# Three Strassen sums and a border's small work moved in a fused retention and two-layer kernel, and the second product's matmuls put behind every second Strassen product

## The chip, the cores and the metric

One Trainium2 chip, one of its cores. The metric is device time in microseconds (us) from launch to end; lower is better. Engines in this text: TensorE (PE, matmuls; PEld its weight loads), VectorE (DVE), ScalarE (ACT), GpSimd (POOL) and SyncE (SP, which issues most DMAs). Matrix results land in PSUM, which has eight banks here called 0 to 7.

## The reference, cut to what matters

```python
B, H, S, D = 4, 8, 576, 64              # 4*576 = 2304 tokens, width 512
scores = q @ k.T / sqrt(D)              # per head
ret = scores * decay(head, i - j)       # retention: a causal decay mask
x = merge_heads(ret @ v)                # (2304, 512)

h = x @ w_in                            # (2304, 2048), first layer
x = relu(h) ** 2 @ w_out                # (2304, 512)

h = x @ w_in2                           # second layer
g = h * clip(h + 3, 0, 6) / 6
out = g @ w_out2                        # (2304, 512)
```

The four weight matrices come in 64-bit floating point; the kernel decodes them on the chip.

## The kernel before

**Precision and passes.** Each operand is split into a high and a low part, so that each product is three passes: high by high, high by low, low by high (`PASSES`). A "low" is always a VectorE or GpSimd subtraction behind a ScalarE copy that makes the "high".

**Stages.** First the retention (until about 60 us), whose result lies in `xall`, feature by token. Then the first layer on the first 768 tokens, directly: 16 steps `c` (`NCH = 16`), each a slice of 128 of the 2048 hidden features. After these come five blocks of 768 tokens (`BLOCKS`; layer 0 for tokens 768 and 1536, then layer 1 for all three), each of which goes through eight pairs of slices (`NPAIR = 8`), 40 pairs `k` in all. In these blocks the first product is made by a Strassen scheme with seven products.

**The first 768 tokens.** In step `c` TensorE runs `emit_h(c)` (24 matmuls into banks 6 and 7, L431) and then the second product of two steps earlier, `firsts(c - 2)` (24 matmuls, L478, in four steps of three 128x512 and three 128x256 ones). ScalarE empties banks 6 and 7 by `relu` (L447), squares (L450) and copies the high part (L451); `emit_h(c + 1)` may not write a bank before its `relu` is done. VectorE makes the low parts (L454) and does the long part of decoding the weights: clamp (L175, L178), `second` (L184), `third` (L190; the name of its tile tells what it is: `w...` for w_in, `wd` for w_out). A decoded slice of w_in is split for `emit_h(c + 2)` by ScalarE (L196) and GpSimd (L197), one of w_out likewise by `split_out`. At odd `c`, `sum_lefts` (L508 to L511) makes the left operands of the Strassen products on VectorE and sends them to DRAM.

**The border to the first Strassen block.** Right operands: four differences T1 to T4 of pieces of `xall` (`sums`, two VectorE operations of 128x384 each, L585), seven high parts on ScalarE (`highs`, L602, two operations each) and seven low parts on VectorE (`lows`, L607). The first pair's left operands for `e` = 2 and 3 are split by `parts_of_left` (L196 on ScalarE, L197 on VectorE).

**A pair.** `pair` runs the seven products in the order P1, P6, P2, P7, P5, P4, P3 (L690, six 128x384 matmuls each), alternately on banks `ta` and `tb` (7 and 6, swapped from pair to pair). P2 adds onto P1's bank after ScalarE has copied P1 out (L725); P7 takes P6's bank after VectorE has made `u2` from it (L714); P4 adds onto P7's bank and P3 onto P5's, each after the L714 on it. The four results become the hidden activations `g` of the pair: in layer 0 by ScalarE (L701, L702, L708) and the low part by VectorE (L710); in layer 1 with L706 and L707 ahead of them. The low part of a result is emitted behind the next product's L714 (`late`, `flush`).

**What stands between the products.** `between(i)` is called after the seven products, `i` = 0 to 6. It emits the matmuls of the second product of the pair before (`pending`, 8 steps in layer 0, L478 with tiles `yps` and `ytail`; 12 steps of three 128x512 matmuls in layer 1, L650), then the side work `side[i]`: loads, the next block's operands, and one "slot" of decoding the second layer's weights (`ready_slots`). The pending steps are those of `e` = 1 first; they need that half's `g`, whose last part comes from P4 of the pair before.

All engines run their instructions strictly in the order in which they are emitted; the lines below are emitted by hand in that order. Nothing is scheduled at run time.

## Time and profile before

| | |
|---|---|
| median of 3 runs | 845.2 us (844.39 to 845.39) |
| profiled execution | 845.26 us, of which the span from first to last instruction is 843.5 us |
| busy: PE / DVE / ACT / POOL | 825.0 / 586.1 / 466.6 / 144.5 us |
| granted TensorE clock | 0.999 of full speed, which is the level of 2.4 GHz |
| DMA | 245 GB/s on average |

A row of the timeline gives the start of a group of equal instructions, how long they were busy, and, in brackets, how long the engine had been idle before and what released it. Matmuls overlap, so the time that TensorE spends on a group is read as the start of the next group less its own start, not as its busy time.

### The profile page before, as it was taken

What the parts mean: (1) busy time and instruction counts of PE and PEld (TensorE: products, weight loads), DVE (VectorE), ACT (ScalarE), POOL (GpSimd) and SP (SyncE); (2) the same over time, 40 slices, a digit from 0 to 9 for tenths busy, and PEclk for the clock granted to TensorE, in tenths of its full rate; (3) what the DMA queues carried; (4) which work ended last, traced back from release to release, by engine and by line L of the source; (5) the groups of instructions that cost most, each with busy time, mean ns of one, the idle gap of its engine ahead of it and who ended that gap; (6) DMA issues with size and microseconds to landing.
All of it is one profiled execution on the core that took longest, in us unless ns stands there. A gap on an engine that the chain in (4) does not pass through costs nothing.

```text
span 843.5 us, 14173 instructions
## 1 busy us (share of the span) xinstructions
PE 825.0 (98%) x5220; PEld 741.9 (88%) x5220; DVE 586.1 (69%) x1018; ACT 466.6 (55%) x913; POOL 144.5 (17%) x122
## 2 busy tenths in 40 slices
PE   8989999997999999999999999999999999999998
PEld 7878888886999899999999888898898888889886
DVE  5779999999787876887875895546644546534434
ACT  1248777768865876867775653335433345433332
POOL 2353333331332320132230130000000000000000
PEclk9999999999999999999999999999999999999999
DMA  9996788876787894689786688553854552854522
GB/s 364 343 300 221 239 289 282 294 249 242 258 326 275 304 330 177 232 280 362 276 293 266 225 287 312 202 185 137 316 221 163 188 199 87 329 209 161 201 99 75
DMA packets 77963, 206.58 MB, mean 245 GB/s; under 512 B 8005, under 2 KB 24773, under 8 KB 77895
## 3 DMA queue, kind: packets, MB, share of 16 engines
q1 hardware_dynamic: 77314, 204.90, 68.9%
q8 instruction: 41, 0.67, 0.3%
q10 hardware_dynamic: 580, 0.79, 0.3%
q14 instruction: 28, 0.22, 0.1%
HBM read 159.00 MB, written 46.66 MB: 244 GB/s over the span
## 4 chain that ended last, share of the span: by engine, by line
PE 80%; DVE 7%; DMA 6%; ACT 4%; issue 1%; SPq 1%; POOL 0%; DVEq 0%; ACTq 0%; POOLq 0%
PE hps L690 33%; PE yps L650 22%; PE yps L478 13%; PE ytail L478 7%; PE hps L431 5%; DMA kvt<-in_kv_dram 3%; DMA qkt<-in_qk_dram 3%; DVE a L184 1%; DVE g L454 1%; DMA stage<-in_w_out_dram 1%; DVE w L190 1%; DVE a L178 1%; ACT u L706 0%; ACT r L172 0%; DVE u L714 0%
## 5 line engine op out<-in xcount | busy, mean ns | idle before, releaser
L650 PE MATMUL yps<-wo,g 128*128 128x512 f32 x864 | 226.8, 394 | 1.5 <-DVE g L710 1.3
L690 PE MATMUL hps<-xlast,win 128*128 128x384 f32 x960 | 194.9, 338 | 1.7 <-DVE u L714 1.6
L650 PEld LDWEIGHTS yps<-wo,g 128*128 128x128 f32 x864 | 159.4, 188 | 26.0 <-DVE g L710 2.0
L690 PEld LDWEIGHTS hps<-xlast,win 128*128 128x128 f32 x960 | 167.7, 188 | 10.5 <-DVE u L714 2.1
L714 DVE TENSOR_TENSOR u<-hps,u 128x384 f32<-128x384 f32 x120 | 66.8, 557 | 157.1 <-PE hps L690 150.5
L478 PE MATMUL yps<-g,wo 128*128 128x512 f32 x576 | 166.1, 396 | 0.4 <-POOL wo L197 0.4
L690 PE MATMUL hps<-xop,win 128*128 128x384 f32 x720 | 146.4, 338 | 3.7 <-ACT r L447 3.4
L690 PEld LDWEIGHTS hps<-xop,win 128*128 128x128 f32 x720 | 125.7, 188 | 10.7 <-ACT r L447 3.6
L708 ACT ACTIVATE g<-c 128x384 fp32r<-128x384 f32 x120 | 63.1, 525 | 88.1 <-DVE c L707 86.6
L478 PEld LDWEIGHTS yps<-g,wo 128*128 128x128 f32 x576 | 101.8, 188 | 10.2 <-POOL wo L197 0.8
L478 PEld LDWEIGHTS ytail<-g,wo 128*128 128x128 f32 x576 | 94.0, 188 | 17.3
L478 PE MATMUL ytail<-g,wo 128*128 128x256 f32 x576 | 98.5, 279 | 0.0
L710 DVE TENSOR_TENSOR g<-c,g 128x384 fp32r<-128x384 f32 x120 | 67.9, 566 | 11.3 <-ACT g L708 11.1
L431 PE MATMUL hps<-xring,win 128*128 128x512 f32 (+1 forms) x384 | 69.7, 338 | 0.3 <-ACT r L447 0.2
L733 ACT ACTIVATE c<-hps 128x384 f32<-128x384 f32 x40 | 19.7, 492 | 90.9 <-PE hps L690 90.9
L431 PEld LDWEIGHTS hps<-xring,win 128*128 128x128 f32 x384 | 60.1, 190 | 8.7 <-ACT r L447 0.7
L706 ACT ACTIVATE u<-c,three 128x384 f32<-128x384 f32 x72 | 44.4, 617 | 31.7 <-DVE c L714 30.5
L714 DVE TENSOR_TENSOR c<-hps,u 128x384 f32<-128x384 f32 x80 | 44.3, 554 | 21.8 <-PE hps L690 21.7
L184 DVE SCALAR_TENSOR_TENSOR a<-stage,a 128x512 int32<-128x512 int32 x64 | 51.2, 800 | 0.9
L707 DVE SCALAR_TENSOR_TENSOR c<-u,c 128x384 f32<-128x384 f32 x72 | 41.3, 574 | 13.5 <-ACT u L706 13.4
L171 ACT ACTIVATE a<-stage 128x512 f32<-128x512 f32 x64 | 42.4, 663 | 6.4 <-DMA stage<-in_w_in_dram 6.4
L172 ACT ACTIVATE r<-stage 128x512 int32<-128x512 uint32 x64 | 42.2, 660 | 0.0
(97 smaller groups left out, 905.5 us busy)
## 6 DMA issues: line engine op xcount, KB each, us to landing
win<-kept SPq DMA_DIRECT2D x88, 512.0 KB
wo<-kept SPq DMA_DIRECT2D x80, 512.0 KB
kept<-ready SPq DMA_DIRECT2D x40, 512.0 KB
win<-kept SPq DMA_DIRECT2D x72, 256.0 KB
stage<-in_w_out_dram SPq DMA_DIRECT2D x32, 512.0 KB
kept<-wo SPq DMA_DIRECT2D x16, 512.0 KB
stage<-in_w_in_dram SPq DMA_DIRECT2D x16, 512.0 KB
qkt<-in_qk_dram SPq DMA_DIRECT2D x13, 512.0 KB
```

Source lines behind the costliest of these rows:

```text
L171: nc.scalar.activation(out=a, in_=high.bitcast(F32), func=ACTF.Abs)
L172: nc.scalar.activation(out=r, in_=low.bitcast(U32), func=ACTF.Copy, scale=2.0 ** -29)
L184: nc.vector.scalar_tensor_tensor(out=a.bitcast(I32), in0=high, scalar=-0x40000000, in1=a.bitcast(I32), op0=ALU.bitwise_and, op1=ALU.bitwis ...
L431: nc.tensor.matmul(out=h, lhsT=w[:, kk // 2, wp, kk % 2 * 128:][:, :128], rhs=xs[kk][xp][:, o:o + n], start=m == 0, stop=m == 3 * KD - 1,)
L478: nc.tensor.matmul(out=p, lhsT=w[:, wp, m * 128:m * 128 + 128], rhs=gt[:, gpart, o:o + n], start=first and e == 0 and not (k and m % 2), s ...
L650: nc.tensor.matmul(out=p, lhsT=gt[:, gpart, m * 128:m * 128 + 128], rhs=w[:, wp], start=first and e == 0, stop=last and e == 2,)
L690: nc.tensor.matmul(out=to, lhsT=wl[k][:, half if k != 1 else 0, wp, o], rhs=x[:, xp, f], start=first and m == 0, stop=last and m == 5, ski ...
L706: nc.scalar.activation(out=v, in_=c, func=ACTF.Relu, bias=three)
L707: nc.vector.scalar_tensor_tensor(out=c, in0=v, scalar=6.0, in1=c, op0=ALU.min, op1=ALU.mult)
L708: nc.scalar.activation(out=hi, in_=c, func=ACTF.Copy)
L710: lambda: nc.vector.tensor_tensor(out=lo, in0=c, in1=hi.bitcast(F32), op=ALU.subtract)
L714: nc.vector.tensor_tensor(out=out_, in0=to, in1=x, op=ALU.add)
```

## The change

Four things are edited.

1. In the 16 steps: T1, T2 and T3 are emitted at the ends of steps 4, 6 and 8 in place of 11, 12 and 13.
2. Steps 13 to 15 and the border: `highs[0]` stands ahead of `split_in(15)` in place of the end of step 13; in step 14 the second w_out decode in hand is finished ahead of `emit_g(14)`; of the two left operands one is split at steps 14 and 15 and the other behind `highs[4]` and `lows[4]`; the last `sum_lefts` goes from step 15 to the end of the border.
3. In the first pair, T4 is emitted at `between(1)` in place of `between(0)`, `highs[5]` and `lows[5]` one place later, and slots begin at `between(3)`, so that the decoding of the second layer's weights, with its loads, stands three places later from there on.
4. In all 40 pairs the second product's steps stand only at those `between(i)` for which 7k + i is odd: behind every second product, counted over all pairs. A pair with even k has three groups of them (after P6, P7 and P4), one with odd k four (after P1, P2, P5 and P3).

```diff
--- before.py
+++ after.py
@@ -931,7 +931,6 @@
         def firsts(c):
             return ywork(wouts[c], g[c], c == 0, c == NCH - 1)
 
-        left_lows = []
 
         def sum_lefts(p):
             whole = left_sums(*(first_in[p][:, e] for e in range(2)), nc.vector)[1]
@@ -952,11 +951,15 @@
                 next_load()
             for d in dec:
                 d.pop(0)()
+            if c == NCH - 2:
+                for d in dec:
+                    for f in d:
+                        f()
+                    next_load()
+                dec = []
             if c == NCH - 1:
                 lows[1]()
-                for f in left_lows:
-                    f()
-                sum_lefts(p)
+                left[0][1]()
             if c > 1:
                 emit_g(c, h)
             for d in dec:
@@ -977,6 +980,8 @@
                 due.append(decode(*halves.pop(0)[1:]))
             for d in due[:1]:
                 d.pop(0)()
+            if c == NCH - 3:
+                highs[0]()
             if c and c + 2 < NCH:
                 split_in(c + 2)
             if c % 2 and c < NCH - 1:
@@ -989,18 +994,14 @@
                 keep(("o", 0, c - LAG), wouts[c - LAG].rearrange("p e n -> p (e n)"))
             if c == NCH - 5:
                 load_left(0)
-            if NCH - 5 <= c < NCH - 2:
-                for f in sums[2 * (c - NCH + 5):][:2]:
+            if c in (4, 6, 8):
+                for f in sums[c - 4:][:2]:
                     f()
-            if c == NCH - 3:
-                highs[0]()
             if c == NCH - 2:
                 highs[1]()
                 lows[0]()
-                for e in (2, 3):
-                    high, low = parts_of_left(0, e)
-                    high()
-                    left_lows.append(low)
+                left = [parts_of_left(0, e) for e in (2, 3)]
+                left[0][0]()
         assert not halves and not due
         pending = firsts(NCH - 2) + firsts(NCH - 1)
         highs[2]()
@@ -1008,7 +1009,10 @@
         lows[2]()
         highs[4]()
         lows[3]()
+        left[1][0]()
         lows[4]()
+        left[1][1]()
+        sum_lefts(NPAIR - 1)
         store_late()
         for c in (NCH - 2, NCH - 1):
             keep(("o", 0, c), wouts[c].rearrange("p e n -> p (e n)"))
@@ -1044,8 +1048,8 @@
                 if j:
                     side[0].append(lows[4])
                 else:
-                    side[0] += sums[6:]
-                for i, at in ((5, 1), (6, 3)):
+                    side[1] += sums[6:]
+                for i, at in ((5, 1 if j else 2), (6, 3)):
                     side[at].append(highs[i])
                     side[at + 1].append(lows[i])
             for i, e in ((4, 1), (6, 0)):
@@ -1057,7 +1061,7 @@
                     for n in range(2):
                         side[i + n].append(lambda e=e, n=n: parts_of_left(k + 1, e)[n]())
             if p < NPAIR - 1:
-                for i in range(4 if j and not p else 0, 7):
+                for i in range(0 if p else 4 if j else 3, 7):
                     if slots:
                         side[i] += [store_late] + slots.pop(0)
             elif late_stores:
@@ -1065,7 +1069,11 @@
             count = len(pending)
 
             def between(i):
-                want = count - count * (i + 1) // 7
+                groups = [n for n in range(7) if (7 * k + n) % 2]
+                if i not in groups:
+                    want = count
+                else:
+                    want = count - count * (groups.index(i) + 1) // len(groups)
                 while len(pending) > want:
                     pending.pop(0)()
                 for f in side[i]:
```

On VectorE, in step 4 of the first 768 tokens (a piece of the difference; `t` is T1's tile):

```order
 L184 SCALAR_TENSOR_TENSOR a<-stage,a 128x512
 L190 ISA w_1327<-a,r 128x1024
+L585 TENSOR_TENSOR t<-xall 128x384 x2
 L175 TENSOR_SCALAR a<-a 128x512
 L178 TENSOR_SCALAR a<-a 128x512
```

T1's two subtractions now stand ahead of the decoding of step 5; T2 and T3 are put in likewise at steps 6 and 8.

On VectorE, the last rows ahead of the first pair's L714 for P6 (`u<-hps,u`), before:

```order
L197 TENSOR_TENSOR win<-win 128x512 x2
L508 TENSOR_TENSOR sums<-w_2119 128x256
L509 TENSOR_TENSOR sums<-sums,w_2119 128x256
L510 TENSOR_TENSOR sums<-w_2119 128x256
L511 TENSOR_TENSOR sums<-w_2119,sums 128x256
L454 TENSOR_TENSOR g<-r,g 128x512
L454 TENSOR_TENSOR g<-r,g 128x256
L607 TENSOR_TENSOR xop<-xall,xop 128x384 x2
L607 TENSOR_TENSOR xlast<-xall,xlast 128x384 x2
L607 TENSOR_TENSOR xlast<-t,xlast 128x384 x2
L585 TENSOR_TENSOR xall<-xall,t 128x384 x2
L714 TENSOR_TENSOR u<-hps,u 128x384
```

and now:

```order
L454 TENSOR_TENSOR g<-r,g 128x512
L454 TENSOR_TENSOR g<-r,g 128x256
L607 TENSOR_TENSOR xop<-xall,xop 128x384 x2
L607 TENSOR_TENSOR xlast<-xall,xlast 128x384 x2
L607 TENSOR_TENSOR xlast<-t,xlast 128x384 x2
L197 TENSOR_TENSOR win<-win 128x512
L508 TENSOR_TENSOR sums<-w_2127 128x256
L509 TENSOR_TENSOR sums<-sums,w_2127 128x256
L510 TENSOR_TENSOR sums<-w_2127 128x256
L511 TENSOR_TENSOR sums<-w_2127,sums 128x256
L714 TENSOR_TENSOR u<-hps,u 128x384
L585 TENSOR_TENSOR xall<-xall,t 128x384 x2
```

One left operand's low part (`win`) and `sum_lefts` went behind the low parts of P2, P7 and P5 (`xop`, `xlast`), and T4 (`xall<-xall,t`) went from ahead of the L714 to behind it.

On TensorE, the pair k = 8, the first of the second block of layer 0 (its P1, P6 and P2 read `xop`, the others `xlast`), before:

```order
L690 MATMUL hps<-xop,win 128x384 x6
L478 MATMUL yps<-g,wo 128x512 x3
L478 MATMUL ytail<-g,wo 128x256 x3
L690 MATMUL hps<-xop,win 128x384 x6
L478 MATMUL yps<-g,wo 128x512 x3
L478 MATMUL ytail<-g,wo 128x256 x3
L690 MATMUL hps<-xop,win 128x384 x6
L478 MATMUL yps<-g,wo 128x512 x3
L478 MATMUL ytail<-g,wo 128x256 x3
L690 MATMUL hps<-xlast,win 128x384 x6
L478 MATMUL yps<-g,wo 128x512 x3
L478 MATMUL ytail<-g,wo 128x256 x3
```

and now:

```order
L690 MATMUL hps<-xop,win 128x384 x12
L478 MATMUL yps<-g,wo 128x512 x3
L478 MATMUL ytail<-g,wo 128x256 x3
L478 MATMUL yps<-g,wo 128x512 x3
L478 MATMUL ytail<-g,wo 128x256 x3
L690 MATMUL hps<-xop,win 128x384 x6
L690 MATMUL hps<-xlast,win 128x384 x6
L478 MATMUL yps<-g,wo 128x512 x3
L478 MATMUL ytail<-g,wo 128x256 x3
L478 MATMUL yps<-g,wo 128x512 x3
L478 MATMUL ytail<-g,wo 128x256 x3
L478 MATMUL yps<-g,wo 128x512 x3
```

A product that stood alone between two steps of the second product now runs right behind another (x12 is two products, one pair of rows `xop` x6 and `xlast` x6 too), and the second product's steps stand two or three together.

## Rows read from the trace of the kernel before

**Rows 1.** Busy time in two stretches (start:end, length, then busy us of each engine).

```profile
core 0: us, PE busy (x) PEld busy (x) DVE busy (x) ACT busy (x) POOL busy (x), PEclk, DMA share, GB/s
85.00:182.00 97.00, 96.79 (x557) 84.92 (x555) 93.54 (x141) 72.56 (x139) 35.57 (x23) 1.00 0.82 275
182.00:203.30 21.30, 15.84 (x85) 13.38 (x85) 20.30 (x37) 14.93 (x32) 4.46 (x3) 1.00 0.53 196
```

**Rows 2.** PE's timeline: `emit_h(15)`, P1 and P7 of the first pair.

```profile
181.98 4.45 PE L431 MATMUL hps<-xring,win 128*128 128x512 f32 x24 [0.21 <-ACT r L447]
...
194.70 1.31 PE L690 MATMUL hps<-xop,win 128*128 128x384 f32 x6 [3.43 <-ACT r L447]
...
203.27 1.32 PE L690 MATMUL hps<-xlast,win 128*128 128x384 f32 x6 [1.56 <-DVE u L714]
```

**Rows 3.** PE's timeline, end of pair 11 and begin of pair 12, layer 0.

```profile
385.43 1.23 PE L690 MATMUL hps<-xlast,win 128*128 128x384 f32 x6
386.49 0.87 PE L478 MATMUL yps<-g,wo 128*128 128x512 f32 x3
...
387.55 0.85 PE L478 MATMUL yps<-g,wo 128*128 128x512 f32 x3
...
388.59 1.21 PE L690 MATMUL hps<-xop,win 128*128 128x384 f32 x6
389.63 0.63 PE L478 MATMUL yps<-g,wo 128*128 128x512 f32 x2
```

**Rows 4.** PE's timeline, pair 26, layer 1.

```profile
612.34 0.86 PE L650 MATMUL yps<-wo,g 128*128 128x512 f32 x3
613.04 1.22 PE L690 MATMUL hps<-xop,win 128*128 128x384 f32 x6
614.10 1.55 PE L650 MATMUL yps<-wo,g 128*128 128x512 f32 x6
615.49 1.21 PE L690 MATMUL hps<-xop,win 128*128 128x384 f32 x6
616.53 1.55 PE L650 MATMUL yps<-wo,g 128*128 128x512 f32 x6
...
625.59 1.55 PE L650 MATMUL yps<-wo,g 128*128 128x512 f32 x6
```

**Rows 5.** DVE's timeline, step 13 to the first pair's L714.

```profile
178.08 0.69 DVE L190 CUSTOM_DVE_ANT_0 w<-a,r 128x1024 uint16<-128x1024 uint16 x1
...
182.21 0.41 DVE L175 TENSOR_SCALAR a<-a 128x512 f32<-128x512 f32 x1
...
190.18 1.12 DVE L175 TENSOR_SCALAR a<-a 128x512 f32<-128x512 f32 x1 [0.32 <-ACT a L171]
...
201.73 1.01 DVE L585 TENSOR_TENSOR xall<-xall,t 128x384 f32<-128x384 f32 x2
202.67 0.55 DVE L714 TENSOR_TENSOR u<-hps,u 128x384 f32<-128x384 f32 x1
```

**Rows 6.** DVE's timeline in step 10: decoded w_in of step 12.

```profile
151.75 0.69 DVE L190 CUSTOM_DVE_ANT_0 w<-a,r 128x1024 uint16<-128x1024 uint16 x1
```

**Rows 7.** PE's timeline: begin of `emit_h(12)`.

```profile
156.47 0.86 PE L431 MATMUL hps<-xring,win 128*128 128x512 f32 x3
```

**Rows 8.** ACT's timeline: `highs[0]`, ahead of the `relu` of step 14.

```profile
180.50 0.94 ACT L602 ACTIVATE xop<-xall 128x384 fp32r<-128x384 f32 x2
```

**Rows 9.** DVE's timeline, end of pair 26: L714 of P3, low part of P4's result.

```profile
625.79 0.56 DVE L714 TENSOR_TENSOR c<-hps,u 128x384 f32<-128x384 f32 x1 [0.57 <-PE hps L690]
626.27 0.55 DVE L710 TENSOR_TENSOR g<-c,g 128x384 fp32r<-128x384 f32 x1
```

**Rows 10.** PE's timeline: behind P3 of pair 18, then behind P1 of pair 19.

```profile
498.46 1.55 PE L650 MATMUL yps<-wo,g 128*128 128x512 f32 x6
...
502.32 0.73 PE L650 MATMUL yps<-wo,g 128*128 128x512 f32 x2 [0.97 <-DVE g L710]
```

**Rows 11.** DVE's timeline at the same place.

```profile
500.70 0.55 DVE L714 TENSOR_TENSOR c<-hps,u 128x384 f32<-128x384 f32 x1
501.17 1.10 DVE L710 TENSOR_TENSOR g<-c,g 128x384 fp32r<-128x384 f32 x1
```

## The prediction

> **What bounds the kernel now.** The busy times by stretch come first: TensorE is busy for 96.79 of 97 us in the first 768 tokens and for 15.84 of 21.30 us at the border [rows 1], so the change can win only at places where TensorE stands still or where its matmuls follow each other more slowly than elsewhere. Its timeline comes next: at the border it waits 3.43 us for ScalarE's `relu` ahead of P1 and 1.56 us for VectorE's L714 ahead of P7, and 0.21 at `emit_h(15)` [rows 2]. VectorE is the engine to look at around there: 93.54 of 97 us busy, then 20.30 of 21.30 [rows 1]; what it does at one place it does not do at another. In the blocks it is mostly the other way: VectorE waits for TensorE there (its rows come below).
>
> **Edit 4, the runs of matmuls.** No matmul is added or removed; the question is what TensorE pays for going from one kind of product to the other. I read start to start. In layer 0, a Strassen product behind one lone step takes 386.49 - 385.43 = 1.06 us; the step of the second product behind it 387.55 - 386.49 = 1.06; a second step in the same run 388.59 - 387.55 = 1.04; and a product behind that run of two 389.63 - 388.59 = 1.04 [rows 3]. In layer 1, a lone step takes 613.04 - 612.34 = 0.70, the product behind it 614.10 - 613.04 = 1.06, a run of two steps 1.39 (so 0.69 for the second), the product behind that 616.53 - 615.49 = 1.04 [rows 4]. So the first of a run is dearer by 0.01 to 0.02, and a product behind a lone step by 0.02, with no wait in either.
>
> A pair of layer 0 has now six lone steps and one run of two; after the change it has 3.5 runs of two or three steps on average. Products: six fall from 1.06 to 1.04, 0.12 (a product right behind another is a case that the trace does not have; its bounds are 1.04, as behind a run of two, and 1.06, as behind a lone step; I take 1.04, since both of its neighbours are then matmuls of 384 columns as inside one product. At 1.06 half of the 0.12 is lost). Steps: 3.5 of them are no longer the first of a run, 3.5 x 0.02 = 0.07, or 3.5 x 0.01 if a third step goes back to 1.05; I take 0.045. Sum 0.165 us for a pair, and the 16 pairs k = 1 to 16 that carry a second product of layer 0 give 2.6 us. A pair of layer 1 has two lone steps and five runs of two, and gets 3.5 runs of three or four: products 2 x 0.02, steps 3.5 x 0.01, less rounding 0.065; the 23 pairs k = 17 to 39 give 1.5 us. **Term: -4.1 us**, between -2.5 (products unmoved in layer 0, steps at the lower value) and -5.0.
>
> The Trainium skill, "TensorE: Matmul & The Clock Gate", section "Wait — 56ns, not 53.3ns?", has a rule against this term: a warm matmul costs its columns at 2.4 GHz and a fixed 2.5 ns, whatever stands ahead of it. Six of 384 columns would then take 0.975 us in every place, a step of layer 0 the same, and the term would be nothing; here they take 1.04 to 1.06 by place, which the rule has no room for.
>
> **Edits 1 to 3, the border.** TensorE loses there the three waits above, and about 0.1 us for the restart behind each: P1's and P7's six matmuls are busy for 1.31 and 1.32 us [rows 2], others for 1.21 to 1.23 [rows 3, 4]. The edits shorten the wait at P1: out of ScalarE's queue ahead of the last `relu` go one left operand's copy, and the wait for VectorE's second decode, which VectorE now finishes ahead of the low parts of g(14). But the last wait of the border is P7's, and that is VectorE's queue: L714 starts at 202.67 [rows 5], P7 at 203.27 [rows 2]. I sum that queue. From 182.21, the first clamp of step 14 [rows 5], VectorE is never idle but for 0.3 us at 190.18 [rows 5]. The work up to L714 is the same list, in another order, less T4 (202.67 - 201.73 = 0.94 [rows 5]), which goes behind it, and one more or one less 0.3. T1 to T3 are no gain there: each is 0.94 too, and since VectorE has no idle time from step 4 on (3.5 us of 97, in pauses too short for one), doing them 7 to 5 steps earlier only makes everything between them later, until at step 13 the queue is where it was: 182.2. So L714 starts about 0.94 + 0.3 = 1.24 us earlier, and P7 at 202.0. On TensorE, however, three steps of the second product stood ahead of P7, and now two do; the third, 1.05 us, comes behind. Gain 1.24 - 1.05 = 0.2.
>
> The delay in the first 768 tokens has its own price. The decoded w_in of step 12 ends at 151.75 + 0.69 = 152.44 [rows 6] and `emit_h(12)` starts at 156.47 [rows 7]: 4.03 us. The shortest such lead that the trace has is the one of step 15: 178.08 + 0.69 = 178.77 [rows 5] to 181.98 [rows 2], 3.21, and there TensorE waited for it, with `highs[0]` on ScalarE in between (0.94 busy [rows 8], 0.83 until the next), so 2.4 is needed. With 3 x 0.94 = 2.8 us the lead of step 12 falls to 1.2, and TensorE stands still for about 1.2 us by then. That is hidden: it waits so much less at P1 and P7, whose time VectorE sets. **Term: -0.2 us**, between -3.0 (VectorE takes in the three sums without falling behind, 2.8 more) and +1.0 (it pays the early stand and keeps the late one).
>
> **Edit 4, the first step of an odd pair.** The pending steps need the low part of P4's result (L710), which stands on VectorE behind the L714 of P3. In a quiet pair: P3's matmuls are through at 625.59 [rows 4], L714 starts at 625.79, L710 ends at 626.27 + 0.55 = 626.82 [rows 9], 1.23 us after P3. Now a run of steps and P1 lie between (1.39 + 1.04, and 0.23 for the first matmul, which needs only the high part): 2.66 us. From an even to an odd pair only P1 is left: 1.04 + 0.23 = 1.27. So the cover goes from 1.4 us to nothing, 12 times in layer 1 (in layer 0 it is 1.06 + 0.24 = 1.30). Where VectorE is late already, P3 itself comes later by the run that went ahead of it, so that the moment at which the step wants L710 stays, and the wait that the trace has there (P3 through at 498.46, L710 done at 502.27, the matmul at 502.32 [rows 10, 11]) stays as it is. Any wait costs the 0.1 of a restart too. Between 0 and 12 x 0.1 = 1.2, at the middle: **term: +0.5 us**. The slots three places later change which decode meets which product; even pairs keep a clamp at `between(4)` and `second` at `between(5)`, as decodes repeat every three slots. I take that at nothing: VectorE's and ScalarE's room in the blocks hides it, and where that is gone a slot's VectorE operation costs its own 0.7 to 0.9 us once.
>
> **Sum.** Against the profiled execution, 845.26 (span 843.5 and 1.8 around it), which is at the median of 845.2: 845.26 - 4.1 - 0.2 + 0.5 = 841.5 us. What a measurement can tell from no change is 0.2%, 1.7 us.
>
> **Rivals.**
> *The pair's end pays it back.* For it: the cover of zero. If every one of the 20 even pairs that an odd one follows costs 0.2 us (a restart and as much of a wait), the term is +4 in place of +0.5: 845.0. Against it: 1.23 is under 1.27.
> *Slower: VectorE's lateness moves with P3.* Until 515 us VectorE starts P3's L714 late: 500.70 against 498.46 + 0.2 in pair 18, 2.0 us [rows 10, 11]; of the ten even pairs up to there each has such a lateness, 0.7 to 2.4 us, and pairs 24 and 32 have 0.8. Their sum is 16.8 us. Today 2.66 us of cover swallow most of it. If it comes from what the products bring, not from the clock, it stays as long when P3 comes later, and nearly all of it is paid; about 2 us are paid already. That gives 841.5 + 14 = 855; it decides from a quarter on, 845. Against it: what stands ahead of that L714 is side work at the same places of the queue, and P3 comes 1.39 us later (layer 1; 2.1 in layer 0) than it did, counted from the pair's begin.
> *The border works.* VectorE swallows the three sums, the lower bound above: 841.5 - 2.8 = 838.7. For it: only the idle 3.5 us of 97; against it: no pause of it is long enough.
> *The order of matmuls does not matter.* If the 0.02 hang on something else that the run does not change (the operands' places, the loads of weights), the first term falls away: 845.6. This is what the rule of the Trainium skill, "TensorE: Matmul & The Clock Gate", would give. Against it: in one pair the same product takes 1.06 and 1.04.
>
> **How the numbers follow.** Forecast (841.5; own range 840.1, the first term at -5.0 and no waits at the pairs' ends, to 844.0, the first at -2.5, 1.2 at the ends and nothing at the border) 0.58; pair's end 0.16; slower 0.10; border works 0.09; no effect of order 0.07. The range takes in the border's rival and the pair's end, and of the last two only the beginning, since the slower one reaches far beyond and the other is small: 838.5 to 845.3. Faster by over 0.2% (under 843.5): nearly all of the forecast (0.55), the border (0.09) and a quarter of the pair's end (0.04), 0.68. Within: the rest of the forecast, most of the pair's end, no effect of order, 0.22. Slower (over 846.9): 0.10.
>
> **What would show it.** Products behind a product, and behind a run of two or three, at 1.04 in both layers; steps at 1.04 and 0.69. P7 of the first pair about 202 us, still released by VectorE's L714, P1 near 192; `emit_h(10)` to `emit_h(12)` waiting for about 1.2 us in all, which today don't wait. First steps of odd pairs with waits under 0.1 us where VectorE isn't late. The prediction is wrong if P7 starts before 200 or after 203.3, if products stay at 1.06, or if waits for L710 by odd pairs add up to more than 4 us.

## The result and the profile after

The changed kernel takes **857.57 us** (median of 4 runs, 855.13 to 858.74) against 845.3 us for the kernel before (844.39 to 846.48): a ratio of 1.0147, 95% interval 1.0126 to 1.0168. The prediction said 841.5. The change made the kernel slower by 1.5%, beyond the upper end of the range, 845.3.

The profiled execution took 858.74 us, its span is 857.0, 13.5 more than before. The first thing to find out is where. A stretch below runs from the start of one pair's P1 to the start of another's, read from TensorE's timeline; pair 0's P1 is at 194.70 us before [rows 2].

| us | P1 of pair 0 at | pair 0 | pairs 1 to 15 | 16 to 19 | 20 to 38 | from P1 of 39 |
|---|---|---|---|---|---|---|
| before | 194.70 | 18.18 | 239.12 | 64.82 | 298.61 | 28.1 |
| after | 193.30 | 21.24 | 244.28 | 69.07 | 300.93 | 28.2 |
| difference | -1.40 | +3.06 | +5.16 | +4.25 | +2.32 | +0.1 |

So every stretch behind the border lost, and the border itself gained 1.4 up to P1. The windows of the changed kernel (columns as in [rows 1]):

```profile
core 0: us, PE busy (x) PEld busy (x) DVE busy (x) ACT busy (x) POOL busy (x), PEclk, DMA share, GB/s
182.00:203.30 21.30, 16.50 (x91) 14.06 (x90) 20.52 (x36) 13.81 (x30) 3.99 (x3) 1.00 0.42 152
199.20:202.40 3.20, 0.24 (x3) 0.03 (x1) 3.17 (x9) 0.49 (x1) 0.00 (x0) 1.00 0.00 0
203.40:206.80 3.40, 3.40 (x11) 2.84 (x10) 1.49 (x3) 1.35 (x3) 0.00 (x0) 0.50 1.02 370
```

TensorE's timeline of the changed kernel at the border, to be set beside [rows 2], with the first matmuls behind P7:

```profile
183.02 4.33 PE L431 MATMUL hps<-xring,win 128*128 128x512 f32 x24
...
193.30 1.49 PE L690 MATMUL hps<-xop,win 128*128 128x384 f32 x7 [1.75 <-ACT r L447]
...
202.38 1.44 PE L690 MATMUL hps<-xlast,win 128*128 128x384 f32 x6 [2.96 <-DVE u L714]
203.61 1.48 PE L478 MATMUL yps<-g,wo 128*128 128x512 f32 x3
204.89 0.84 PE L478 MATMUL ytail<-g,wo 128*128 128x256 f32 x3
```

`emit_h(15)` comes 1.04 us later, P1 waits 1.75 in place of 3.43, and P7 starts 0.89 earlier than in [rows 2]; its L714 on VectorE starts at 201.77, where [rows 5] has 202.67. Unforeseen is the last row of the windows: the granted clock is 0.50, the level of 1.2 GHz, for 3.4 us behind P7's wait. Three matmuls of 512 columns take 204.89 - 203.61 = 1.28 us there, and 0.70 at the full clock [rows 4].

The runs of matmuls in layer 0 (TensorE, pair 11, to be set beside [rows 3]), then in layer 1 (pairs 25 and 27, beside [rows 4]):

```profile
385.36 2.25 PE L690 MATMUL hps<-xlast,win 128*128 128x384 f32 x12
387.44 0.86 PE L478 MATMUL yps<-g,wo 128*128 128x512 f32 x3
...
388.49 0.85 PE L478 MATMUL yps<-g,wo 128*128 128x512 f32 x3
...
389.53 2.25 PE L690 MATMUL hps<-xlast,win 128*128 128x384 f32 x12
...
614.98 2.27 PE L690 MATMUL hps<-xlast,win 128*128 128x384 f32 x12
617.09 2.24 PE L650 MATMUL yps<-wo,g 128*128 128x512 f32 x9
619.17 2.27 PE L690 MATMUL hps<-xlast,win 128*128 128x384 f32 x12
...
640.06 2.34 PE L650 MATMUL yps<-wo,g 128*128 128x512 f32 x9
642.24 2.27 PE L690 MATMUL hps<-xop,win 128*128 128x384 f32 x12
```

In layer 0 two products take 2.08 (1.04 each), two steps 2.09. In layer 1 two products take 2.11 and nine matmuls 2.08, but the nine at 640.06, an odd pair's first run, take 2.18: one restart of 0.1. Quiet pairs (start of P1 to start of P1): layer 0 15.85 before and 15.67 after for even k; layer 1 15.69 before, 15.67 after for even k and 15.78 for odd k.

What is not quiet are the odd pairs of layer 0: 16.33 to 17.05, eight of them 134.4 in all, 9.0 more than 8 x 15.67. Some waits are old: pairs 5 and 9 took 16.98 and 16.05 before. One of the odd pairs, pair 7, on TensorE and then, from the end of pair 6, on VectorE and ScalarE:

```profile
311.68 1.21 PE L690 MATMUL hps<-xop,win 128*128 128x384 f32 x6
313.04 0.51 PE L478 MATMUL yps<-g,wo 128*128 128x512 f32 x1 [0.16 <-ACT g L708]
313.77 0.73 PE L478 MATMUL yps<-g,wo 128*128 128x512 f32 x2 [0.23 <-DVE g L710]
...
308.89 1.07 DVE L175 TENSOR_SCALAR a<-a 128x512 f32<-128x512 f32 x1 [1.22 <-ACT a L171]
...
311.49 0.69 DVE L197 TENSOR_TENSOR win<-win 128x512 fp32r<-128x512 f32 x1
312.10 0.68 DVE L184 SCALAR_TENSOR_TENSOR a<-stage,a 128x512 int32<-128x512 int32 x1
312.70 0.55 DVE L714 TENSOR_TENSOR c<-hps,u 128x384 f32<-128x384 f32 x1
313.17 0.55 DVE L710 TENSOR_TENSOR g<-c,g 128x384 fp32r<-128x384 f32 x1
...
312.46 0.52 ACT L708 ACTIVATE g<-c 128x384 fp32r<-128x384 f32 x1
```

P3's matmuls are through at 311.68, where P1 begins. VectorE has a left operand's low part and a decoding step ahead of P3's L714, starts it 1.0 us after that, and the L710 behind it ends at 313.72; TensorE goes on at 313.77, where a run of three matmuls was to start at 312.72. The same place before, VectorE and then TensorE:

```profile
304.58 1.07 DVE L175 TENSOR_SCALAR a<-a 128x512 f32<-128x512 f32 x1 [0.57 <-ACT a L171]
...
308.41 0.55 DVE L714 TENSOR_TENSOR c<-hps,u 128x384 f32<-128x384 f32 x1
308.88 0.55 DVE L710 TENSOR_TENSOR g<-c,g 128x384 fp32r<-128x384 f32 x1
...
309.12 1.21 PE L690 MATMUL hps<-xop,win 128*128 128x384 f32 x6
310.17 0.86 PE L478 MATMUL yps<-g,wo 128*128 128x512 f32 x3
```

Pair 6's P1 starts at 293.27 there and at 295.93 in the changed kernel. Counted from it, the clamp (L175) starts at 11.31 before and at 12.96 now, and L710 is done at 16.16 before and at 17.79 now, while the second matmul of the first step, the first to need it, is due at 17.12 before and at 17.02 now. Of the 9.0 us of the eight pairs, about 6 lie at this first step and about 3 between P6 and the step behind P2, where P2 waits for ScalarE's copy of P1 (L725).

All waits of TensorE for L710 (us in total, times, longest), before and then now:

```profile
PE yps L650 <- DVE g L710: 1.3, 2, 1.0
...
PE yps L650 <- DVE g L710: 3.3, 4, 1.6
PE yps L478 <- DVE g L710: 2.4, 7, 0.6
```

In pairs 25 and 33 the same wait stands alone; in pair 24 no decoding is left on VectorE, and what stands ahead of P3's L714 are two copies of the second product's result (L663):

```profile
608.50 2.12 PE L650 MATMUL yps<-wo,g 128*128 128x512 f32 x8 [0.59 <-DVE g L710]
735.38 2.11 PE L650 MATMUL yps<-wo,g 128*128 128x512 f32 x8 [0.59 <-DVE g L710]
```

### The profile page after: what moved, and what is told of

Same layout as the page of the kernel before. It is cut to its first block, busy times and chain, and to the rows that moved or that the text cites. A ratio compares the mean times of both kernels' runs of the same rounds, so it can differ in the third digit from the quotient of the medians.

```text
span 857.0 us, 14184 instructions
## 1 busy us (share of the span) xinstructions
PE 831.1 (97%) x5220; PEld 739.6 (86%) x5220; DVE 585.9 (68%) x1018; ACT 464.7 (54%) x913; POOL 142.5 (17%) x122
## 4 chain that ended last, share of the span: by engine, by line
PE 55%; DVE 17%; ACT 11%; DMA 10%; issue 4%; POOL 1%; SPq 1%; DVEq 0%; ACTq 0%; POOLq 0%
PE hps L690 25%; PE yps L650 21%; PE yps L478 5%; DMA kept<-ready 3%; DMA kvt<-in_kv_dram 3%; PE ytail L478 3%; DVE a L184 3%; DVE g L454 2%; DMA stage<-in_w_in_dram 2%; DVE wd L190 2%; ACT a L171 1%; DMA kept<-wo 1%; ACT r L172 1%; DVE a L175 1%; ACT ready L196 1%
## 5 line engine op out<-in xcount | busy, mean ns | idle before, releaser
L650 PE MATMUL yps<-wo,g 128*128 128x512 f32 x864 | 214.3, 394 | 3.8 <-DVE g L710 3.3
L690 PE MATMUL hps<-xlast,win 128*128 128x384 f32 x960 | 184.2, 336 | 3.0 <-DVE u L714 3.0
L478 PE MATMUL yps<-g,wo 128*128 128x512 f32 x576 | 169.0, 399 | 3.3 <-DVE g L710 2.4
L714 DVE TENSOR_TENSOR u<-hps,u 128x384 f32<-128x384 f32 x120 | 66.6, 555 | 151.1 <-PE hps L690 149.1
L690 PE MATMUL hps<-xop,win 128*128 128x384 f32 x720 | 143.0, 339 | 4.7 <-ACT r L447 1.8
L478 PEld LDWEIGHTS yps<-g,wo 128*128 128x128 f32 x576 | 98.7, 190 | 16.6 <-DVE g L710 5.2
L708 ACT ACTIVATE g<-c 128x384 fp32r<-128x384 f32 x120 | 63.1, 526 | 80.5 <-DVE c L707 79.0
L710 DVE TENSOR_TENSOR g<-c,g 128x384 fp32r<-128x384 f32 x120 | 66.5, 554 | 13.6 <-ACT g L708 11.9
L714 DVE TENSOR_TENSOR c<-hps,u 128x384 f32<-128x384 f32 x80 | 44.2, 552 | 24.7 <-PE hps L690 24.7
L184 DVE SCALAR_TENSOR_TENSOR a<-stage,a 128x512 int32<-128x512 int32 x64 | 49.4, 773 | 0.8
L171 ACT ACTIVATE a<-stage 128x512 f32<-128x512 f32 x64 | 42.3, 661 | 4.7 <-DMA stage<-in_w_in_dram 4.7
L175 DVE TENSOR_SCALAR a<-a 128x512 f32<-128x512 f32 x64 | 39.1, 611 | 5.0 <-ACT a L171 5.0
```

Of the source, the lines that this page charges most:

```text
L171: nc.scalar.activation(out=a, in_=high.bitcast(F32), func=ACTF.Abs)
L175: nc.vector.tensor_scalar(out=a, in0=a, scalar1=LEAST, scalar2=MOST, op0=ALU.max, op1=ALU.min)
L184: nc.vector.scalar_tensor_tensor(out=a.bitcast(I32), in0=high, scalar=-0x40000000, in1=a.bitcast(I32), op0=ALU.bitwise_and, op1=ALU.bitwis ...
L478: nc.tensor.matmul(out=p, lhsT=w[:, wp, m * 128:m * 128 + 128], rhs=gt[:, gpart, o:o + n], start=first and e == 0 and not (k and m % 2), s ...
L650: nc.tensor.matmul(out=p, lhsT=gt[:, gpart, m * 128:m * 128 + 128], rhs=w[:, wp], start=first and e == 0, stop=last and e == 2,)
L690: nc.tensor.matmul(out=to, lhsT=wl[k][:, half if k != 1 else 0, wp, o], rhs=x[:, xp, f], start=first and m == 0, stop=last and m == 5, ski ...
```

## The experiments

All of them in one table first, stretches as above, from the profiled execution of each; the paragraphs below say what each name stands for. Between profiled executions the start of the first step's matmuls moves from 61.4 to 64.8 us, so the stretches tell more than the span. The granted clock is 0.50 for 3.4 us (6.8 us in edit 4, shift by one and copy first) somewhere from 192 to 208 us in all of them but the kernel before, edits 1 to 3, border only and pair 0 spread, so small differences in the column of pair 0 say little.

| | ratio to before (interval) | P1 of pair 0 | pair 0 | 1 to 15 | 16 to 19 | 20 to 38 |
|---|---|---|---|---|---|---|
| edits 1 to 3 | 1.0088 (1.0059 to 1.0116) | 192.01 | 18.71 | 242.20 | 68.54 | 298.17 |
| edit 4 | 1.0108 (1.0085 to 1.0130) | 193.54 | 19.14 | 241.62 | 66.79 | 300.91 |
| after P3 too | 1.0067 (1.0047 to 1.0087) | 193.90 | 17.34 | 241.59 | 66.34 | 300.93 |
| low first | 1.0221 (1.0193 to 1.0249) | 190.98 | 21.02 | 246.96 | 69.36 | 301.54 |
| P3 alone | 1.0002 (0.9986 to 1.0019) | 193.20 | 19.11 | 239.02 | 64.45 | 298.43 |
| border only | 1.0007 (0.9991 to 1.0023) | 193.07 | 18.69 | 241.76 | 64.83 | 298.52 |
| shift only | 1.0045 (1.0029 to 1.0062) | 194.02 | 18.15 | 239.76 | 68.62 | 298.07 |
| light decoding | 1.0084 (1.0063 to 1.0104) | 192.59 | 21.23 | 239.05 | 65.85 | 300.91 |
| edits 1 to 3, P3 alone | 1.0082 (1.0063 to 1.0101) | 192.23 | 19.63 | 242.02 | 68.17 | 298.43 |
| border, P3 alone | 1.0020 (1.0007 to 1.0032) | 192.21 | 21.18 | 238.90 | 64.48 | 298.42 |
| pair 0 spread | 1.0136 (1.0118 to 1.0154) | 192.19 | 18.71 | 247.09 | 69.05 | 300.90 |
| runs where quiet | 1.0009 (0.9999 to 1.0018) | 194.58 | 18.16 | 237.99 | 65.53 | 298.02 |
| shift by one | one run | 195.56 | 18.74 | 249.55 | 63.86 | 298.02 |
| shift by two | one run | 194.89 | 18.15 | 243.46 | 65.39 | 298.73 |
| shift, copy first | one run | 193.70 | 18.57 | 240.08 | 66.75 | 298.30 |

**Edits 1 to 3 alone** (the changed kernel with the old `between`).

```diff
-                groups = [n for n in range(7) if (7 * k + n) % 2]
...
+                want = count - count * (i + 1) // 7
```

> The changed kernel with the second product's steps spread over all seven places again, so edits 1 to 3 alone. Theory (the loss is edit 4: from an even to an odd pair only P1 stands between P3 and the first pending step, and VectorE's low part L710 comes too late for it): 843 to 846 us, since P7 of the first pair is held by VectorE's L714 near 202 us as in the changed kernel (202.38), with three steps ahead of it in place of two, and the pairs run as before. Rival (the border and the shifted slots cost it): 850 us or more, with waits in the pairs up to k = 19 as in the changed kernel. If the half clock behind the long wait at P7 belongs to the border, a stretch near 203 us shows it here too, and costs 1 to 2 us.

850.37 us (849.46 to 853.06) against 843.63: missed, and on the rival's side. Up to P1 it gains 2.7 us (1.4 of it ahead of the first step, where executions differ anyway), and pairs 1 to 19 lose 6.8. What the prediction put at nothing, the slots and the border's shadow in the blocks, costs half of the loss by itself.

**Edit 4 alone** (the kernel before with the new `between`).

> The kernel before with edit 4 alone: the second product's steps behind every second product, the border and the slots as before. Theory (edit 4 is the loss): 853 to 857 us, odd pairs 0.5 to 1.2 us longer than before in layer 0, 0.1 in the quiet pairs of layer 1. Rival (border and slots): 841 to 844, the gain of 2.6 us or so of the runs alone.

852.9 us (851.97 to 854.11) against 843.63, just under the lower end of what was expected: edit 4 brings the larger part of the loss. All of the +2.3 in pairs 20 to 38 is its own (300.91), and the quiet even pairs of layer 0 are at 15.67.

**Steps behind P1, P2, P5 and P3 of every pair**, on the kernel before: `groups = [0, 2, 4, 6]`.

> The kernel before with four groups in every pair, behind P1, P6 with P2, P7 with P5, and P4 with P3: every pair then ends with a group, as the odd pairs of the changed kernel do, and no pair begins its pending steps with P1 alone behind P3. Theory (the missing cover between P3 and the first pending step): the waits for L710 fall away, odd and even pairs take 15.67 to 15.75 us in layer 0, and the whole 841 to 845 us. Rival (any grouping by two makes results come in twos and ScalarE and VectorE late): 849 us or more, with waits in even and odd pairs alike.

849.66 us (848.83 to 850.0), on the rival's side. The first pending step has its cover back, a run of steps and P1, but P4 and P3 come as a couple at the end of every pair, and the cover does not always do: pairs 7, 11 and 13 still wait 0.23 to 0.42 us for L710, pairs 17 and 19 0.62 and 1.03. Pairs 1, 5 and 9 wait for ScalarE's L725 (0.17 to 0.91), which stands behind the results of P4 and P3, and pairs 24 and 32 wait 0.91 for a right operand's low part, L607. That pairs 20 to 38 have 300.93 as in the changed kernel is chance.

**The low part ahead of P3's sum**, in the changed kernel: `flush()` ahead of `add(c12, ta, u2)`.

> The changed kernel with one thing in another order on VectorE: the low part of P4's result (L710) ahead of the L714 of P3, so that it no longer waits for P3. Theory: 849 to 853 us; the 0.1 us at each quiet odd pair of layer 1 is gone (L710 done long before), the waits for L710 in layer 0 shrink by up to 0.5 us each, and what is left is where VectorE or ScalarE are late anyway, and the wait of P2 for the copy of P1 (L725). Rival (L710's place behind P3 does not matter, VectorE is simply late by its side work): within 2 us of 857.6.

863.31 us (859.69 to 863.76): missed on the wrong side. The quiet odd pairs of layer 1 did fall from 15.78 to 15.68, so the restart there was L710's, and TensorE's waits for L710 fell from 5.7 to 1.2 us in all. But VectorE's queue now waits for ScalarE's L708 ahead of P3's sum, everything behind it is later, and TensorE's waits for L725 rose from 1.1 to 8.8 us.

**Steps behind P6, P7, P4 and P3 of every pair**, on the kernel before: `groups = [1, 3, 5, 6]`. A run of steps now stands on both sides of P3, and P1 and P6 ahead of the first pending step.

> The kernel before with the second product's steps behind P6, P7, P4 and P3 of every pair (four groups in each pair, P3 alone between two of them), no other edit. Theory (a group of two products by itself does no harm; what costs is a pair whose P4 and P3 stand together ahead of one run of steps, and a first pending step with only P1 ahead of it): here P3's result has a run of steps, P1 and P6 ahead of the step that wants it, each bank's reader 3.1 us, so no new wait; the pairs of layer 0 go from 15.85 to 15.67 us, those of layer 1 stay within 0.03: 16 x 0.18 = 2.9 under the kernel before, 839.5 to 843. Rival (any grouping by two makes ScalarE's and VectorE's work come in bunches): odd and even pairs of layer 0 at 16.2 and more, 848 or more.

844.43 us (843.05 to 848.82) against 845.0: over the theory's range, and the rival falls too. Twos as such cost nothing in the time, and pairs 20 to 38 are at 298.43, 2.5 us under edit 4's, without one wait. (P4 and P3 as a couple, which the expectation names, stand at the end of the odd pairs; from an even pair to an odd one it is P3 and P1.) The gain of the quiet pairs, 15.65, is eaten above all by pairs 1, 3, 5, 9 and 17, at 16.31 to 16.92: the waits of 0.3 us and more that the profile names in them are 0.75, 0.97 and 0.39 us (pairs 3, 5 and 17) for VectorE's L714 ahead of P7 and 0.58 (pair 9) for ScalarE's L725.

**The border's edits without the slots' shift and without edit 4.**

```diff
-                for i in range(0 if p else 4 if j else 3, 7):
+                for i in range(4 if j and not p else 0, 7):
```

> The border's edits 1 and 2 and T4's place of edit 3, without the slots' shift by three and without edit 4. Theory (what the three edits together lost, 6.7 us, comes from the shift of the slots, which puts other decoding steps behind each product): pairs 1 to 19 as in the kernel before, the border as predicted, 842.5 to 845.5. Rival (the loss comes from the border's order, T4 and the late low parts): 849 or more.

845.42 us (843.18 to 847.27) against 845.0, as expected: no change that can be measured. P1 is 1.6 us earlier than in [rows 2], and pair 1, which was expected to stay, gives it back at 18.30 in place of 15.85: TensorE waits there 0.57 us for a load of second-product weights (`wo<-kept`) and 1.08 for L725.

**The slots' shift alone**, on the kernel before: the same line the other way.

> The kernel before with the slots beginning at the fourth place of the first pair, nothing else. Theory (the shift is what edits 1 to 3 lose): pairs 1 to 19 lose 5 to 7 us, 848 to 851. Rival (the shift costs only together with the border's order): within 1.7 us of the kernel before.

848.73 us (847.66 to 849.14), as expected in time; but what is lost in the trace, 3.8 us, lies in pairs 16 to 19 and not in the fifteen before them. TensorE in pair 17, and ScalarE ahead of it:

```profile
473.72 1.33 PE L690 MATMUL hps<-xop,win 128*128 128x384 f32 x6 [1.02 <-ACT u L725]
...
472.07 0.66 ACT L171 ACTIVATE a<-stage 128x512 f32<-128x512 f32 x1
472.62 0.67 ACT L172 ACTIVATE r<-stage 128x512 int32<-128x512 uint32 x1
473.18 0.49 ACT L725 ACTIVATE u<-hps 128x384 f32<-128x384 f32 x1
```

The begin of a decoding (two copies, L171 and L172) now stands ahead of P1's copy, for which P2 waits.

**The changed kernel with light decoding**: three of the four VectorE operations of the second layer's decoding are left out, so it computes with other weights.

```diff
         def clamp():
+            if l:
+                return
...
         def second():
+            if l:
+                return
```

> The changed kernel without the clamp and the joining of the sign in the decoding of the second layer's weights (three of VectorE's four operations for each of 32 half slices are left out, so the second layer computes with other weights). Theory (VectorE's side work, at its old places of the queue, is what keeps it late while the results come in twos): the odd pairs of layer 0 fall to 15.8 or less, pairs 17 to 19 to 16.2 or less; 844 to 849 with the first pair still at 20 us. Rival (the bunches on ScalarE alone, relu, square and copy of two results in a row, make the waits): odd pairs of layer 0 stay at 16.3 or more, 853 or more.

851.87 us (850.34 to 853.23): between the two. Pairs 1 to 15 fall from 244.28 to 239.05, 16 to 19 from 69.07 to 65.85; odd pairs of layer 0 are at 16.08 to 16.42. The place of pair 7 that was shown above (VectorE, then TensorE; L718 and L714 are here what are L714 and L710 elsewhere, four lines down):

```profile
309.59 0.56 DVE L718 TENSOR_TENSOR c<-hps,u 128x384 f32<-128x384 f32 x1 [0.86 <-PE hps L694]
310.06 0.55 DVE L714 TENSOR_TENSOR g<-c,g 128x384 fp32r<-128x384 f32 x1
...
310.43 0.97 PE L482 MATMUL yps<-g,wo 128*128 128x512 f32 x3
311.24 0.51 PE L482 MATMUL ytail<-g,wo 128*128 128x256 f32 x3
```

VectorE waits for TensorE again, and the first step runs through but for a restart (0.81 us to the next group in place of 0.70). So VectorE's side work was what made it late: at the first steps of layer 0's odd pairs the loss falls from about 6 us to about 1. About 0.4 us in each of these pairs, P2's wait for L725 on ScalarE, stays and is the rival's share. The 0.59 us in pairs 25 and 33 stay too: no decoding stood there.

**Edits 1 to 3 with `groups = [1, 3, 5, 6]`.**

> The changed kernel (edits 1 to 3 as they are) with the steps behind P6, P7, P4 and P3 of every pair in place of edit 4's alternation. Theory (edit 4 loses by its odd pairs, where the first step and P2 have too little between them and the work they wait for; edits 1 to 3 lose for themselves): what is left is the loss of edits 1 to 3 alone, 850.4, less up to 3 us of the quiet pairs: 847 to 851; pairs 20 to 38 at 298.5 us. Rival (the lateness of VectorE that the border and the shift bring makes any grouping dear): 854 or more.

851.14 us (849.51 to 852.92), at the upper end of the theory, just outside: edit 4's loss goes, 298.43 in pairs 20 to 38, and that of edits 1 to 3 stays, 68.17 in pairs 16 to 19. The quiet pairs' gain is not seen in the time.

**The border's edits and `groups = [1, 3, 5, 6]`, slots not shifted.**

> The border's edits without the slots' shift, and the steps behind P6, P7, P4 and P3 of every pair: the two parts that alone left the time as it was. Theory (they don't touch each other): 843 to 846.5. Rival (the border's lateness in pair 1 and the groups add to each other): 849 or more.

845.39 us (844.15 to 848.94) against 844.5: as expected, and no faster than the kernel before.

**Pair 0 with its old spread**, the rest as in the changed kernel: `groups = ... if k else list(range(7))`.

> The changed kernel, but pair 0 keeps the steps of the kernel before, one to seven places; all other pairs as edit 4 has them. Theory (pair 0 lost 3 us since three steps fewer stand ahead of P7 and TensorE's clock fell to half behind the longer wait): pair 0 falls from 21.2 to about 18.7, 854 to 856. Rival (pair 0's loss is the border's own): within 1 us of the changed kernel.

855.92 us (855.42 to 857.89), inside the expected time, for another reason than expected. Pair 0 falls from 21.24 to 18.71 and the clock is 1.00 all through 182 to 220 us, but pairs 1 to 15 rise from 244.28 to 247.09, pair 1 alone from 16.56 to 18.45. TensorE in pair 1:

```profile
212.76 0.49 PE L478 MATMUL yps<-g,wo 128*128 128x512 f32 x1 [0.65 <-ACT g L708]
213.50 0.74 PE L478 MATMUL yps<-g,wo 128*128 128x512 f32 x2 [0.24 <-DVE g L710]
217.75 1.32 PE L690 MATMUL hps<-xop,win 128*128 128x384 f32 x6 [1.06 <-ACT u L725]
```

What TensorE doesn't lose at the half clock it waits for ScalarE and VectorE 10 us later. The two ratios can't be told apart, so the rival has it: pair 0's price is not what made the kernel slower.

**Groups only where they met no wait**, on the kernel before: `[1, 3, 5, 6] if k in (2, 4, 6, 7, 8, 10, 11, 13, 14, 15, 16) else list(range(7))`.

> The kernel before, with the steps behind P6, P7, P4 and P3 in pairs 2, 4, 6, 7, 8, 10, 11, 13, 14, 15 and 16 alone, where such groups met no wait. Theory (0.2 us each for a quiet pair of layer 0): 2.2 us under the kernel before, a ratio of 0.997 to 0.998. Rival (the gain of a pair only brings the next late work of VectorE or ScalarE into sight): a ratio of 0.999 or more.

844.8 us (844.05 to 846.15) against 844.5: the rival. Pairs 1 to 15 do gain 1.1, and pairs 16 to 19 give 0.7 of it back. No version that was run beats the kernel before.

**The slots shifted by one and by two**, and **by three with the slot at the end of pairs 16 and 18 put behind the next pair's P1**, on the kernel before. The shifts are the line of the slots' shift with 1 and 2 in place of 3; the last edit, against the shift by three alone:

```diff
+                if k in (17, 19):
+                    side[0] += [store_late] + slots.pop(0)
-                for i in range(0 if p else 4 if j else 3, 7):
+                for i in range(0 if p else 4 if j else 3, 6 if k in (16, 18) else 7):
```

> The kernel before with the slots one place later instead of three, nothing else. Theory (a shift costs by what it puts ahead of a copy or a sum that TensorE waits for: at three places the begin of a decoding, two copies of 0.55 us on ScalarE, stands at the end of pairs 16 and 18, ahead of the next pair's P1 copy L725; at one place none stands there): pairs 16 to 19 at 64.5 to 66 us. Rival (the slots end later, and any delay costs by its length): 1.3 us for one place, 66.1 or more, and 67.3 for two.

> The kernel before with the slots two places later. Theory: the begins of decodings stand at the end of pairs 17 and 19, so pair 18 or 20 waits for L725 and pairs 17 and 19 don't; pairs 16 to 19 at 65.5 to 67. Rival (costs by length): 67.3.

> The kernel with the shift by three alone, but the slot at the end of pairs 16 and 18 goes behind the next pair's P1, so that ScalarE makes P1's copy L725 ahead of the decoding's two copies, and VectorE the last L710 ahead of the decoding's last operation. Theory (place in the queue): the waits for L725 in pairs 17 and 19 (1.02 and 0.47 us) go, pairs 16 to 19 fall from 68.6 to 67.3 or less. Rival (VectorE is late by its whole list, so the wait moves to the next product): 68 to 69.

One run each, 855.54, 850.43 and 847.22 us, beside 846.15 for the kernel before. The length of the delay is out as the cause: pairs 16 to 19 take 63.86 for one place, less than before, 65.39 for two, 68.62 for three. The first is a little under what was expected, the second inside it; not expected is that a shift by one loses 10.4 us in pairs 1 to 15 and one by two 4.3. With P1's copy put back ahead (L725 at 472.50, L171 at 472.87), pair 17 falls from 17.56 to 16.45 and pair 19 from 18.09 to 17.35, 1.9 for the four pairs as expected; the other 1.9 of the shift stay. The edit also put VectorE's L710 ahead of the slot's decoding step, so the 1.9 are not the copies' alone for certain. The shift by one: TensorE's waits in pairs 9, 11, 13 and 15, then VectorE ahead of the second.

```profile
345.29 1.22 PE L478 MATMUL yps<-g,wo 128*128 128x512 f32 x2 [2.53 <-DVE g L710]
380.88 0.73 PE L478 MATMUL yps<-g,wo 128*128 128x512 f32 x2 [2.20 <-DVE g L710]
415.03 0.73 PE L478 MATMUL yps<-g,wo 128*128 128x512 f32 x2 [2.20 <-DVE g L710]
449.20 0.72 PE L478 MATMUL yps<-g,wo 128*128 128x512 f32 x2 [2.19 <-DVE g L710]
...
376.94 1.23 DVE L197 TENSOR_TENSOR win<-win 128x512 fp32r<-128x512 f32 x1
378.08 0.95 DVE L175 TENSOR_SCALAR a<-a 128x512 f32<-128x512 f32 x1
379.07 0.83 DVE L178 TENSOR_SCALAR a<-a 128x512 int32<-128x512 int32 x1
379.82 0.55 DVE L714 TENSOR_TENSOR c<-hps,u 128x384 f32<-128x384 f32 x1
```

One place on, the clamp falls behind a left operand's low part and ahead of P3's sum, at the end of the pairs before these: 2.9 us of side work ahead of the sum on which the next pair's first step hangs.

## Why the prediction was wrong

**The runs of matmuls** (term -4.1). Right in layer 0: 0.18 us a quiet pair where 0.165 was worked out, and a product behind a product takes 1.04. In layer 1 too large: 0.02 in place of 0.065; two products take 2.11 there, not twice 1.04. Were every pair quiet, it would be 16 x 0.18 + 23 x 0.02 = 3.3 us. By the fixed 2.5 ns for each warm matmul that the Trainium skill, "TensorE: Matmul & The Clock Gate", section "Wait — 56ns, not 53.3ns?", gives for matmuls back to back, quiet pairs would have stayed as they were; the trace differs in layer 0 (15.85 to 15.67) and nearly agrees in layer 1 (15.69 to 15.67). But that gain is not a gain in time: the groups on both sides of P3 keep it in the quiet pairs and end within the measurement of the kernel before, and groups at quiet places alone do no better.

**The border** (term -0.2). The queue was summed nearly right: L714 0.90 us earlier for 1.24, P7 at 202.38 for "about 202", still released by L714, and 1.04 us later at `emit_h(15)` for the 1.2 that were said to be hidden. P1 came at 193.30 for 192. No term had the half clock behind P7: pair 1's P1 starts 1.7 us later than before, where 0.2 earlier was worked out. Border edits alone leave the time as it is.

**The first step of an odd pair** (term +0.5). This is the step that failed, in its second half. In a quiet pair the price is the restart, 0.1, the upper end of what was given. Where VectorE is late already, the prediction said that "the moment at which the step wants L710 stays", and that the wait therefore stays as it is. The moment does stay (17.12 us after pair 6's P1 before, 17.02 now), but L710 does not end where it did (16.16 before, 17.79 now). The side work between the results of P5 and P3 comes later than before, the clamp by 1.65 us, and the cover that had swallowed the lateness (2.66 us in layer 1, 3.4 in layer 0) had become 1.3. TensorE's waits for L710 grow from 1.3 to 5.7 us, more than the 4 us that were named as a sign of being wrong. That side work makes the lateness is shown: with three of four decoding operations gone, the 9.0 us of the odd pairs fall to 129.3 - 8 x 15.67 = 4.0. Why the list comes later is not taken apart: P5 and P4 now run as a couple, and P5's L714 in pair 6 starts 1.0 us later after P1 (10.72 for 9.72), but VectorE then also waits 1.22 us for ScalarE's L171, for 0.57 before. Pairs 25 and 33 show the wait alone, 16.9 us for 16.05 and 15.89.

It was nearest to the slower rival's mechanism, at 855, which was given 0.10, but that the time came out close to its number is partly luck. The rival let the lateness stay as long when P3 comes later. Measured as the prediction did (L714's start less P3's end and 0.2), the lateness of the twelve pairs that the rival counts adds up to 16.3 us before (16.8 in its sum), 7.0 under edit 4 alone and 10.1 in the changed kernel. It stays in pairs 24 and 32 (0.75 before, 0.76 now); in pairs 2, 10, 12 and 14 it is gone under edit 4 alone, as the prediction's argument would have it. The rest of the time comes from two things that the rival missed: P2's wait for ScalarE's L725 in odd pairs, some 0.4 each in layer 0, and the next point.

**The slots three places later, "taken at nothing".** Alone they cost 1.0045 (1.0029 to 1.0062), 3.8 us in pairs 16 to 19. The argument was one of room, with one VectorE operation as the price where it ends; what counts is what stands ahead of L725 and L714 in a queue at the end of a pair, and that repeats. Half of the 3.8 went when the slot at such a place, with its two copies ahead of L725, was moved (one run); the other half is not taken apart.

Between them: edit 4 alone 9.3 us over its kernel before, edits 1 to 3 alone 6.7, the two together 12.3. They add up but for 3.7 us, which fits waits that swallow each other, as pair 0 and pair 1 do in the run with the old spread; that sum was not tested by itself.

## What to carry to other kernels

Count the cover of every wait on the slack that the late engine really has, not on a quiet pair. When an edit moves the products that an engine waits for, work out anew at what moment that engine ends its list, and not only at what moment the consumer wants the result: here the second stayed and the first did not. Side work that repeats with one period in a schedule of another has good and bad phases; a shift by one place can cost more than one by three, so price it by listing what stands ahead of each instruction that the bounding engine waits for. And time gained on the bounding engine in stretches where another engine catches up is given back some microseconds later.

## What the runs showed of the hardware

The granted clock fell to the 1.2 GHz level for 3.4 us behind P7's wait, in which TensorE had been busy for 0.24 of 3.2 us; two steps that take about 1.05 us each elsewhere took 3.57 there (203.61 to 207.18), 1.5 us lost. It does not follow from the length of a wait alone: before, TensorE stood still for 3.43 us ahead of P1 [rows 2], and the granted clock is 1.00 from 192 to 208 us there. In the same stretch, 192 to 208 us, the profiled runs of edits 1 to 3, of the border alone and of the old spread in pair 0 have 1.00, those of the groups around P3, of the shift alone and of the kernel with groups at quiet places 0.89; the ratios of these kernels do not go by it. Nor is the half clock the changed kernel's alone: the mean granted clock over a whole run lies between 0.996 and 0.998 in its four runs, and between 0.995 and 1.000 in 23 runs of the kernel before.
